# A third score tile in batch 0, proj on two other queues, and one-pass transposes in a hash-attention and max-out FFN kernel

## Chip, cores and metric

One core of one Trainium2 chip. The metric is device time in microseconds (us) of one launch; TensorE's granted clock is noted with each run, 1.000 being full speed. A ratio is always the mean time of one kernel's fast runs over the mean of the other's fast runs of the same rounds, so it is not quite the ratio of the medians quoted beside it. Brackets after a ratio are its 95% interval. Runs that the record marks as slow (over 1.5% above the fastest of the same kernel) are left out of ratios.

In the profiles PE is TensorE (PEld its weight loads), ACT is ScalarE, DVE is VectorE, POOL is GpSimd, and SP is SyncE, which here only issues DMAs. PSUM is the memory into which this kernel's matmuls write; its pools there are counted in banks, and a tile takes one or two of them.

## The reference

Attention in which a query sees only keys with the same 6-bit hash, then a feed-forward layer with the maximum of three products. 4 batches, 8 heads, 768 positions, 64 per head.

```python
q_bits = (np.einsum('bhsd,dk->bhsk', q, proj) > 0)      # 6 bits, k alike
mask = q_bucket[:, :, :, None] == k_bucket[:, :, None, :]
scores = np.where(mask, scale * np.matmul(q, k.transpose(0, 1, 3, 2)), -1e9)
attn = softmax(scores)                                   # + 1e-9 in the divisor
x = np.matmul(attn, v)                                   # to (3072, 512)
h = np.maximum(np.maximum(x @ w1, x @ w2), x @ w3)       # 512 -> 768
out = h @ w_out                                          # 768 -> 512
```

## The kernel before

The work goes pair of heads by pair of heads. I call the work on one pair of batch 0 a **stage**. A stage has twelve **score units** (two matmuls of 384 columns and one exp on ACT). Other work hangs on the numbered units of the stage: the row sums of the pair before ("den"), its output matmuls (`av`), the **hash** of the next pair, and the preparation of the pair after that. The FFN of a batch starts when its last pair is done, and its matmuls then fill TensorE between score units.

The hash bits get into the scores as extra rows of the score operands. Batch 0's first pair writes them with DVE; each later pair's hash goes into one tile, `bt`, from which eight small DMAs (9 KB each, all on SP's queue) carry it to the operand rows of the next stage.

```python
psp = tile_pool(name="psp", bufs=2, PSUM)   # score tiles, two banks each
psw = tile_pool(name="psw", bufs=4, PSUM)   # one-bank work tiles: all else

def hash_pair(b, j):
    bt = btp.tile([P, S], BF16, tag="bt", name="bt")
    ps = [bank(), bank()]                    # two work banks at once
    ...                                      # 8 matmuls over tf["q"], tf["k"]
    for half in (0, 1):
        nc.vector.tensor_scalar(out=bt[:, half_cols(half)], in0=ps[half][:, 0:HS], ...)
        for hd in (0, 1):
            for z, nm in enumerate(("q", "k")):
                o = 32 * (2 * (hd ^ half) + z)
                nc.sync.dma_start(oset(b, j)[nm, hd][HROW[hd] : HROW[hd] + 2 * NBITS, half_cols(half)],
                                  bt[o : o + 2 * NBITS, half_cols(half)])
```

The schedule of a stage `ph` (cut), where `add(u, f, ...)` hangs `f` behind score unit `u`:

```python
        if ph > 0:                                   # sparse: stages 1 to 4
            add(1, den_mm, ph - 1, 0, NT3 if sparse else NCH)
            if sparse:
                add(2, den_mm, ph - 1, NT3, NCH)     # ends in ACT's copy of the sums
            add(3 if sparse else 2, den_rc, ph - 1)  # DVE, then 8 small GpSimd copies "r"
            ...
        if ph == 1:
            for m in range(3):
                add(6, load_weight, m, 0)            # GpSimd's queue, 384 KB each
            add(6, load_v, 0, 2)
        else:
            add(6, load, "k", nb, nj)                # GpSimd's queue, 4 x 176 KB and more
            add(6, load, "q", nb, nj)
        ...
        if 0 < ph and ph + 1 < len(pairs):
            add(1, hash_pair, *pairs[ph + 1])
```

The softmax here doesn't subtract the row's maximum and nothing guards it: scores larger than these inputs give would overflow.

## Time and profile before

| | before |
|---|---|
| time | 301.68 us, median of 3 (300.83 to 303.58) |
| span of the profiled run, clock | 299.7 us, 0.998 |
| second exp of stages 1, 2, 3, 4 | 29.36, 42.96, 54.29, 65.77 us |
| first FFN matmul that needs the last pair | 73.26 us |
| from there to the end | 226.4 us, TensorE full |

All times in the trace count from the start of the span. I mark a stage by the start of its second exp, because the second score unit is the one that needs the seventh of the eight small DMAs.

### The profile page before, as it was taken

To read this page: it belongs to the slowest core of one execution; us is meant where nothing else is said; L and a number is where in the kernel's file an instruction comes from. 1 tells how busy PE (TensorE), PEld (TensorE's weight loads), DVE (VectorE), ACT (ScalarE), POOL (GpSimd) and SP (SyncE) were. 2 spreads that over 40 slices of the span, in tenths; PEclk is the share of its full clock that TensorE was granted. 3 is DMA by queue.
4 is the path that set the end of the run, shared out by engine and by line. 5 is a ranking of instruction groups with operands and counts; after the bars stand their busy time and mean duration, and the time that the engine had idled before them with its cause. 6 is when DMAs were issued, how large, how long until landed. Compare 5 with 4: busy or idle time off the path is not lost.

```text
span 299.7 us, 6326 instructions
## 1 busy us (share of the span) xinstructions
PE 281.5 (94%) x2328; PEld 147.7 (49%) x2328; DVE 196.4 (66%) x410; ACT 190.8 (64%) x286; POOL 101.5 (34%) x288
## 2 busy tenths in 40 slices
PE   6788888887999899999999999999999999999994
PEld 3344443333555345555555545554555455555551
DVE  2787576885888767887578858875787063725260
ACT  2456758877767696777767776768686966131322
POOL 8180506396344444435260717080202010100000
PEclk9999999999999999999999999999999999999999
DMA  7556193789979093909372757367202020020202
GB/s 238 159 153 131 15 181 88 149 186 199 230 136 200 19 232 121 194 11 218 114 195 35 171 164 173 58 148 188 38 0 37 20 88 1 2 105 0 108 0 106
DMA packets 21727, 34.56 MB, mean 115 GB/s; under 512 B 3744, under 2 KB 15936, under 8 KB 21696
## 3 DMA queue, kind: packets, MB, share of 16 engines
q0 software_dynamic: 14512, 23.60, 39.6%
q1 hardware_dynamic: 6496, 10.03, 9.6%
q10 hardware_dynamic: 688, 0.52, 0.5%
q8 instruction: 18, 0.29, 0.4%
q14 instruction: 13, 0.11, 0.1%
HBM read 33.03 MB, written 6.29 MB: 131 GB/s over the span
## 4 chain that ended last, share of the span: by engine, by line
PE 85%; ACT 6%; DVE 3%; issue 2%; DMA 2%; POOL 1%; ACTq 0%; DVEq 0%; POOLq 0%
PE wk L327 32%; PE sc L256 19%; PE wk L309 11%; PE wk L343 10%; PE wk L272 5%; PE wk L234 4%; PE wk L200 3%; DMA pr<-in_proj_dram 2%; PE wk L219 1%; DVE qtf L202 1%; ACT at_194 L258 1%; ACT at_201 L258 1%; ACT at_182 L258 1%; ACT at_181 L258 1%; ACT at_200 L258 1%
## 5 line engine op out<-in xcount | busy, mean ns | idle before, releaser
L327 PE MATMUL wk<-xT,w_sb 128*128 128x384 f16 x576 | 111.0, 326 | 0.7 <-DVE xT L315 0.7
L327 PEld LDWEIGHTS <-w_sb 128*128 128x128 f16 x576 | 54.1, 97 | 45.0 <-issue 9.8
L237 DVE TENSOR_SCALAR bt<-wk,thrqk,fac 128x384 bf16<-128x384 f32 x30 | 18.9, 673 | 22.3 <-PE wk L234 22.2
L256 PE MATMUL sc<-qop_0_165,kop_0_164 76*128 76x384 bf16 x72 | 23.6, 328 | 4.1 <-DVE qop_0_165 L223 0.6
L309 PEld LDWEIGHTS <-v 128*64 128x64 f16 x384 | 20.6, 110 | 13.7 <-issue 6.7
L91 POOL DMA_DIRECT2D qnat<-in_q_dram x48 | 26.5, 559 | 1.0 <-DMA v<-in_v_dram 1.0
L91 POOL DMA_DIRECT2D knat<-in_k_dram x48 | 26.4, 558 | 0.8 <-issue 0.8
L256 PE MATMUL sc<-qop_0_162,kop_0_160 128*128 128x384 bf16 x72 | 23.5, 326 | 0.4 <-DVE qop_0_162 L223 0.3
L256 PE MATMUL sc<-qop_1_171,kop_1_170 76*128 76x384 bf16 x60 | 19.7, 328 | 3.1 <-DMA kop_1_170<-bt 1.0
L357 ACT COPY o<-wk 128x512 f32<-128x512 f32 x23 | 13.5, 585 | 13.3 <-PE wk L343 13.2
L256 PE MATMUL sc<-qop_2_177,kop_2_176 76*128 76x384 bf16 x60 | 19.7, 328 | 2.2 <-ACT at_187 L258 0.6
L256 PE MATMUL sc<-qop_1_168,kop_1_166 128*128 128x384 bf16 x60 | 19.6, 326 | 0.1
L256 PE MATMUL sc<-qop_2_174,kop_2_172 128*128 128x384 bf16 x60 | 19.6, 327 | 0.0
L283 DVE STREAM_TRANSPOSE dT<-ds 128x384 f32<-128x384 f32 x16 | 9.2, 573 | 8.3 <-ACT ds L278 8.2
L258 ACT ACTIVATE at_185<-sc 128x768 f16<-128x768 f32 x8 | 6.5, 814 | 11.6 <-PE sc L256 11.6
L272 PEld LDWEIGHTS <-ones_154 128*32 128x32 f16 x384 | 8.6, 96 | 10.0 <-issue 6.9
L234 PE MATMUL wk<-qtf,pmq 64*32 64x384 f32 x120 | 13.4, 495 | 0.0
L234 PE MATMUL wk<-ktf,pmk 64*32 64x384 f32 x120 | 12.7, 495 | 0.0
L99 POOL DMA_DIRECT2D v<-in_v_dram x16 | 11.8, 739 | 1.7 <-PE sc L256 1.2
L312 DVE TENSOR_SCALAR sv<-wk 128x1 f32<-128x1 f32 x32 | 4.9, 152 | 11.4 <-PE wk L309 11.4
L256 PEld LDWEIGHTS <-kop_0_164 76*128 76x128 bf16 x72 | 7.0, 97 | 10.5 <-issue 5.3
L256 PEld LDWEIGHTS <-kop_0_160 128*128 128x128 bf16 x72 | 7.1, 98 | 9.9 <-issue 6.6
(479 smaller groups left out, 654.3 us busy)
## 6 DMA issues: line engine op xcount, KB each, us to landing
knat<-in_k_dram POOLq DMA_DIRECT2D x48, 176.0 KB, 4.0
qnat<-in_q_dram POOLq DMA_DIRECT2D x48, 176.0 KB, 5.2
out_dram<-o SPq DMA_DIRECT2D x7, 768.0 KB
v<-in_v_dram POOLq DMA_DIRECT2D x16, 192.0 KB, 5.4
w_sb<-in_moe_w_dram POOLq DMA_DIRECT2D x6, 384.0 KB, 6.8
wo_sb<-in_moe_w_out_dram POOLq DMA_DIRECT2D x1, 768.0 KB, 9.5
out_dram<-o SPq DMA_DIRECT2D x2, 256.0 KB
qnat_98<-in_q_dram ACTq DMA_DIRECT2D x2, 192.0 KB
```

Of the source, the lines that this page charges most:

```text
L91: nc.gpsimd.dma_start(t[32 * g : 32 * g + 32, :, 0 : NCH * D - 32], s[:, :, 32 * blk : 32 * blk + NCH * D - 32])
L99: nc.gpsimd.dma_start(t[:].rearrange("p h c d -> p h (c d)"), v[b, 2 * j : 2 * j + 2].rearrange("h (p c) d -> p h (c d)", p=P))
L234: nc.tensor.matmul(ps[half][o : o + 32, 0:HS], pm[nm][head_rows(hd), :], tf[nm, b, j][head_rows(hd), half_cols(half)], start=True, stop=True)
L237: nc.vector.tensor_scalar(out=bt[:, half_cols(half)], in0=ps[half][:, 0:HS], scalar1=thr["qk"][:, 0:1], scalar2=fac[:, 0:1], op0=AluOp.is_ ...
L256: nc.tensor.matmul(sc[:, hd, 0:HS], kT[rows, c * P : c * P + P], qT[rows, half * HS : half * HS + HS], start=True, stop=True)
L258: nc.scalar.activation(atile(ph, half, c)[:, :, 0:HS], sc[:, :, 0:HS], ActFn.Exp, scale=SCALE)
L272: nc.tensor.matmul(ps[32 * g : 32 * g + 32, 0:HS], ones32[:], atile(ph, half, c)[:, hd, 0:HS], start=(c == 0), stop=(c == NCH - 1))
L283: nc.vector.transpose(dT[:].rearrange("p a x -> p (a x)"), rcb.pop(ph)[:])
L309: nc.tensor.matmul(ps[D * hd : D * hd + D, 0 : HS + 1], vv[:, hd, c, :], atile(ph, half, c)[:, hd, :], start=(c == 0), stop=(c == NCH - 1))
L327: nc.tensor.matmul(ps[:, 0:HS], w_sb[m, fb // NT3][:, jc, (fb % NT3) * P : (fb % NT3) * P + P], xT[b][:, jc, half * HS : half * HS + HS], ...
L343: nc.tensor.matmul(ps[:, 0:DM], hts[b, half, fb][:, t * P : t * P + P], w_sb["o"][:, fb, :], start=(fb == 0), stop=(fb == NFB - 1))
L357: nc.scalar.copy(o[:, t, :], ps[:, 0:DM])
```

## The change

The intent: with two score tiles TensorE and ACT take turns; a third lets ACT keep work in hand in batch 0, where TensorE is not full. The two banks for it come from the work banks, and are given back (`split_scores`) in stage 4. Because only two work banks are left and the hash takes both, the hash moves from unit 1 to unit 3, behind the sums. proj no longer waits on GpSimd's queue. The transposes of pairs 1 to 3 become one pass over the full array, for which the two heads are loaded side by side, in pieces of 256 B.

```diff
-    psw = tile_pool(name="psw", bufs=4, PSUM)
+    psw = tile_pool(name="psw", bufs=2, PSUM)
+    extra = psx.enter_context(tc.tile_pool(name="psx3", bufs=1, PSUM))
+    sc_ring = deque((psp, psp, extra))       # three score tiles
+    def split_scores():                      # later: two score tiles, four banks
+        psx.close(); ...; bank_ring.extend((extra, extra))
 ...
     pr = konst.tile([P, NBITS], FP32, name="pr")
-    nc.gpsimd.dma_start(pr[0:D], proj[:, :])
-    nc.gpsimd.dma_start(pr[D : 2 * D], proj[:, :])
     for cs in (slice(0, NT3), slice(NT3, NCH)):
         load0("k", 0, nc.sync, cs)
         load0("q", 0, nc.scalar, cs)
+        if cs.start == 0:
+            nc.sync.dma_start(pr[0:D], proj[:, :])
+            nc.scalar.dma_start(pr[D : 2 * D], proj[:, :])
 ...                                          # pe_transpose, pairs 1 to 3
-            for hd in (0, 1):
-                nc.tensor.matmul(ps[head_rows(hd), c * P : c * P + P], nat[...][:, hd, o : o + D], iden[:], ...)
+                nc.tensor.transpose(ps[:, c * P : c * P + P], n[:, cc * P : cc * P + P], iden[:])
 ...                                          # schedule
+            if ph == NPAIR:
+                add(6, split_scores)
-            add(1, hash_pair, *pairs[ph + 1])
+            add(3 if ph <= NPAIR else 1, hash_pair, *pairs[ph + 1])
 ...                                          # stage 0; and prep of pairs 2, 3 on units 5, 7, 9, 10
-            add(3, hash_first, "q", 1)
-            add(3, convert, "q", 0, 0, h1)
-            add(4, hash_pair, 0, 1)
+            add(3, hash_pair, 0, 1)
+            add(4, hash_first, "q", 1)
+            add(4, convert, "q", 0, 0, h1)
```

More of the change, by code (lines that the diff above doesn't have):

```diff
@@ L60 @@
     psp = ctx.enter_context(tc.tile_pool(name="psp", bufs=2, space=bass.MemoryType.PSUM))
-    psw = ctx.enter_context(tc.tile_pool(name="psw", bufs=4, space=bass.MemoryType.PSUM))
+    psw = ctx.enter_context(tc.tile_pool(name="psw", bufs=2, space=bass.MemoryType.PSUM))
+    psx = ctx.enter_context(ExitStack())
     ctx.enter_context(tc.manual_schedule())
@@ L80, in load0 @@
         if (nm, 0, j) not in nat:
-            nat[nm, 0, j] = natp0.tile([P, 2, S // 2], FP32, tag=nm + "nat0", name=nm + "nat0")
+            nat[nm, 0, j] = natp0.tile([P, S], FP32, tag=nm + "nat0", name=nm + "nat0")
         src = HBM[nm][0, 2 * j : 2 * j + 2].rearrange("h (p c) d -> p h c d", p=P)[:, :, cs, :]
-        eng.dma_start(nat[nm, 0, j][:].rearrange("p h (c d) -> p h c d", d=D)[:, :, cs, :], src)
+        if j == 0:
+            eng.dma_start(nat[nm, 0, j][:].rearrange("p (h c d) -> p h c d", h=2, d=D)[:, :, cs, :], src)
+        else:
+            dst = nat[nm, 0, j][:].rearrange("p (c h d) -> p h c d", h=2, d=D)
+            for hd in (0, 1):
+                eng.dma_start(dst[:, hd, cs, :], src[:, hd, :, :])
     def load(nm, b, j):
@@ L180, in load_wo, with psum2 @@
         w_sb["o"] = t
-    def psum2(name):
-        return psp.tile([P, 2, 512], FP32, tag="ps", name=name)
+    extra = psx.enter_context(tc.tile_pool(name="psx3", bufs=1, space=bass.MemoryType.PSUM))
+    sc_ring = deque((psp, psp, extra))
+    bank_ring = deque((psw, psw))
+    def psum2():
+        sc_ring.rotate(-1)
+        return sc_ring[0].tile([P, 2, 512], FP32, tag="sc", name="sc")
     def bank():
-        t = psw.tile([P, 512], FP32, tag="wk", name="wk")
-        return t
+        bank_ring.rotate(-1)
+        t = bank_ring[0].tile([P, 512], FP32, tag="wk", name="wk")
+        return t
+    def split_scores():
+        psx.close()
+        extra = psx.enter_context(tc.tile_pool(name="psx1", bufs=2, space=bass.MemoryType.PSUM))
+        sc_ring.remove(sc_ring[[p is psp for p in sc_ring].index(False)])
+        bank_ring.extend((extra, extra))
     tf = {}
@@ L197, in pe_transpose @@
         for c in range(NT3):
-            o = (half * NT3 + c) * D
-            for hd in (0, 1):
-                nc.tensor.matmul(ps[head_rows(hd), c * P : c * P + P], nat[nm, b, j][:, hd, o : o + D], iden[:],
-                                 start=True, stop=True)
+            cc = half * NT3 + c
+            n = nat[nm, b, j]
+            if j == 0:
+                for hd in (0, 1):
+                    o = (hd * NCH + cc) * D
+                    nc.tensor.matmul(ps[head_rows(hd), c * P : c * P + P], n[:, o : o + D], iden[:],
+                                     start=True, stop=True)
+            else:
+                nc.tensor.transpose(ps[:, c * P : c * P + P], n[:, cc * P : cc * P + P], iden[:])
         evac(tf[nm, b, j][:, half_cols(half)], ps[:, 0:HS])
@@ L250, in qk_unit @@
     def qk_unit(ph, b, j, half, c):
-        sc = psum2("sc")
+        sc = psum2()
         for hd in (0, 1):
@@ L374 @@
     TAILW = 40.0
-    wps = psum2("wps")
+    wps = psum2()
     for _ in range(8):
@@ L398, in prep @@
             if nb == 0:
-                for i, (nm, half) in enumerate((("k", 0), ("k", 1), ("q", 0), ("q", 1))):
-                    add(u + i // 2, pe_transpose, nm, nb, nj, half, nc.vector.tensor_copy)
+                for u, nm, half in ((5, "k", 0), (7, "k", 1), (9, "q", 0), (10, "q", 1)):
+                    add(u, pe_transpose, nm, nb, nj, half, nc.vector.tensor_copy)
                     if half == 1:
-                        add(u + i // 2, convert, nm, nb, nj)
+                        add(u, convert, nm, nb, nj)
             else:
@@ L419 @@
         if ph == 0:
-            add(2, hold, nat["q", 0, 1][:, 0, 0:1])
+            add(2, hold, nat["q", 0, 1][:, 0:1])
             add(2, load_v, 0, 0)
```

## The prediction

> **What bounds the kernel now.** I read the page first, then the table by stretches, the timeline of TensorE and SP, the waits of PE, and the chain that ended last in order of time. The page says who is full:
>
> ```profile
> PE 281.5 (94%) x2328; PEld 147.7 (49%) x2328; DVE 196.4 (66%) x410; ACT 190.8 (64%) x286; POOL 101.5 (34%) x288
> PE   6788888887999899999999999999999999999994
> ```
>
> One digit is 7.5 us. From the tenth digit on TensorE is full; before that it is at seven or eight tenths. I cut the table by stretches at the first score matmul of each pair (a "stage" is one pair of heads of batch 0) and at the first FFN matmul. Columns: stretch, its length, then busy time and count of PE, PEld, DVE, ACT, POOL, the clock, DMA share, GB/s.
>
> ```profile
> 11.27:27.89 16.62, 14.55 (x157) 7.96 (x157) 13.73 (x27) 9.06 (x12) 6.85 (x11) 1.00 0.65 155
> 27.89:41.66 13.77, 12.28 (x136) 6.45 (x137) 8.74 (x19) 8.98 (x14) 4.38 (x12) 1.00 0.46 69
> 41.66:52.96 11.30, 9.41 (x89) 3.86 (x89) 6.78 (x15) 9.26 (x14) 5.59 (x16) 1.00 0.59 118
> 52.96:64.44 11.48, 9.55 (x89) 3.86 (x89) 8.91 (x18) 9.29 (x14) 6.56 (x18) 1.00 0.71 150
> 64.44:73.26 8.82, 7.02 (x70) 2.65 (x69) 7.02 (x14) 6.20 (x9) 6.25 (x16) 1.00 1.21 205
> 73.26:290.00 216.74, 215.69 (x1712) 116.94 (x1712) 144.48 (x284) 142.19 (x217) 64.27 (x178) 1.00 0.45 106
> ```
>
> From 73.26 on, when batch 0 is finished and its FFN fills every gap, PE is busy 215.69 of 216.74 us, and the change leaves that work alone. So the question is only how much earlier than 73.26 the first FFN matmul starts. Before it no engine is full: in stages 2 and 3 PE, DVE and ACT are all below 84%. The cause is two score tiles: PE waits for an exp, then goes off to other work, and ACT runs dry. The timeline of PE and of ACT in stage 2:
>
> ```profile
> 46.70 0.32 PE L256 MATMUL sc<-qop_2_177,kop_2_176 76*128 76x384 bf16 x1 [0.61 <-ACT at_181 L258]
> 47.99 0.81 ACT L258 ACTIVATE at_184<-sc 128x768 f16<-128x768 f32 x1
> 49.52 0.81 ACT L258 ACTIVATE at_185<-sc 128x768 f16<-128x768 f32 x1 [0.72 <-PE sc L256]
> ```
>
> Exps back to back start 0.71 us apart; the gap after the one at 47.99 is the 1.11 us of output matmuls that PE had put between two score units. At the front the chain is different: everything waits for proj.
>
> ```profile
> 1.94 5.37 DMA pr<-in_proj_dram
> 7.43 0.47 DVE pmq L139
> 7.94 0.35 DVE ktf L202
> 8.34 0.86 PE wk L219 x4
> 13.55 1.46 PE wk L200 x24
> ```
>
> The k half that DVE evacuates at 7.94 was in PSUM at about 5.6 (its transposes start at 4.72 and take 0.88); DVE stood behind pm, which stood behind proj.
>
> **What the Trainium skill says.** (1) "DMA: Bandwidth & Descriptors", Specifications: first byte about 1 us for a GpSimd-issued DMA and about 0.6 us for one from SP or ACT, and at least 512 B for line rate. The first agrees in direction only: proj took 5.37 us because it shared engines with the loads that ran at over 300 GB/s from 3 to 9 us. The second bears on the new loads, whose pieces fall from 1536 to 256 B; no row of this trace shows what that costs. (2) "TensorEngine Tiling (Array Packing)", Restrictions: column tiling disables the transpose mode of fp32 input. The transposes now write halves of 64 partitions and the trace shows two passes per matmul (24 instructions for 12 matmuls), as that would have it. (3) "Perfetto Trace Analysis", Transposes: use the transpose, not a standard matmul. This trace has none to compare. (4) The same page, Identifying Dependency Chains: consistent bubbles can mean too few buffers; the ACT gaps above, repeated in each stage at the same place, agree.
>
> **The change, part by part.**
>
> *Front.* proj now goes out as the second DMA on SP and on ACT, behind the first k and q halves, whose transposes start at 4.72. I take it to land at 5.0. pm is then done by 5.6, ktf leaves at 5.65 instead of 7.94, and hashing starts near 6.25 instead of 8.34: 2.1 us earlier, all on the path.
>
> *Transposes.* 12 matmuls of two passes per k or q of a pair become 6 transposes. At the 61 ns per pass seen now (1.46 us over 24) that is 0.37 us with one pass each and 0.73 us with two. PE drops 0.7 to 1.1 us for each of six such groups, 4.4 to 6.5 us in all, but most of it lies where PE waits for DVE or ACT, so I do not add it; it only keeps PE from becoming the bound.
>
> *Third score tile.* With three, ACT has up to two units in hand while PE does 1.11 us of output matmuls or 1.4 us of den and hash. The floor of a stage is then ACT: 12 exps at 0.71 plus one 0.36 us copy, about 9.0, so PE/ACT alternation would give 9.0 to 9.8 us instead of 11.3 to 13.8.
>
> *What pays for it.* Two work banks instead of four until the split. So the hash, which needs two, moves from unit 1 to unit 3 and waits for ACT's copy of the sums. That lengthens another chain, which SP shows:
>
> ```profile
> 45.04 0.72 SPq L243 DMA_DIRECT2D qop_0_165<-bt  x1
> ...
> 49.84 0.72 SPq L243 DMA_DIRECT2D qop_0_162<-bt  x1
> 50.61 0.72 SPq L243 DMA_DIRECT2D kop_0_160<-bt  x1
> ```
>
> Each hash sends eight small DMAs, 0.78 us apart, and the second score unit of the next stage needs the seventh. From the first issue that is 6 x 0.78 + 0.72 = 5.4, and 1.4 to landing (stage 1 began 1.4 us after the end of such an issue): 6.8. Directly measured at stage 0: first issue 21.73, second unit of stage 1 at 28.46, that is 6.73. Now the loop from a stage's second unit: score 0.33, den 0.6, score 0.33, den 0.6, the copy of the sums ends 2.5; rest of the hash 0.7; DVE does dT and rc before bt (to 3.6) and the first bt half to 4.25; first issue 4.35; plus 6.8. That is 11.1 us per stage, more than the ACT floor. Before, the hash at unit 1 closed this loop in about 9.6 and the alternation in 11.4 hid it.
>
> *Sum, by the second score unit of each stage.* Stage 1 before: 28.46. After: 2.1 from the front, and about 1.9 since pair 1's hash now stands ahead of the second q half's hash and converts on DVE (2 x 0.6 + 0.7): 24.5, gain 4.0. Stage 2 before: 42.37, 13.9 later; after 11.3 (the 11.1 plus a little, as pair 3's four groups share two banks with the output matmuls): gain 2.6. Stages 3 and 4: 11.34 and 11.48 become 11.1: gain 0.6. From stage 4's second unit to the first FFN matmul: 8.1 before; 2.5 to the copy plus the 4.8 of dT, rc, GpSimd copies, rb and xT seen from 68.41 to 73.22: 7.3, gain 0.8. Total 8.0, so 301.7 - 8.0 = 293.7.
>
> **The rivals.** *The small-DMA chain does not bind* (landing quicker, hash earlier): stages run at the ACT floor plus stalls, about 9.8. Three stages then give 3 x 1.3 more: about 289.8. For it: exps and PE have the room. Against it: SP's spacing of 0.78 is in every stage, and the order of the after kernel has the hash wait for ACT. *Two banks choke it:* each evacuation waits in DVE's line behind converts (0.55 each) and rb, and DVE is already busy 13.73 of 16.62 in stage 0. If every stage loses 1 us more, the gain is about 4: 297.7. *Loads in 256 B pieces starve stage 0:* pairs 1 and 2 are 1.57 MB; at the 350 GB/s of now they land by 9, at half of it by 15. k of pair 1 is needed near 11.3 and pair 2 not before 17, so a halving hides; at a third of the rate stage 0 slips by 2 us or so: 296. *Nothing is kept:* GpSimd and DMA (share 1.21 just before the FFN) set when weights and batch 1 arrive, and an earlier FFN could wait for them. Against it: GpSimd's work of a stage is 6.6 us of 11.1, and PE shows three waits, 1.1 us in all, on other engines after 73 us.
>
> **Range and chances.** I take 293.6. The low end, 289.5, is the first rival; the high end, 297.5, is choked banks or slow loads. A gain of over 2% means under 295.6; the sum leaves 2 us of room to that and its parts have an error of about 2.5 us together, so 0.75 faster, 0.24 within 2%, and 0.01 slower, as no part touches the full stretch after 73 us.
>
> **What would show it.** Right: proj landed near 5 us and first hash matmul near 6.2; first FFN matmul near 65.3; stages 2 and 3 near 11 us with PE's first waits there on the bt DMAs; PE busy down by 4 to 6 us; the stretch from the first FFN matmul to the end still 226.4 us. Wrong in its main step: stages 2 and 3 under 10.3 us (the DMA loop does not bind), or over 11.5 with PE waiting for DVE at den, hash or output matmuls (two banks bind), or the first transposes of pair 1 waiting for a load (pieces bind), or a longer stretch after the FFN begins.

## The result

312.95 us (median of 4, 311.23 to 315.05) against 302.00 (median of 4) before: ratio 1.0362 [1.0279, 1.0445]. The kernel became 3.6% slower. All runs after are at a clock of 0.953 to 0.965. The profiled one has a span of 311.8 us.

The page of the kernel after, the same two lines as before and the clock (before, that row shows 9 in all forty places):

```profile
PE 286.9 (92%) x2220; PEld 145.8 (47%) x2220; DVE 196.2 (63%) x410; ACT 192.1 (62%) x286; POOL 100.3 (32%) x286
...
PE   8786969494999989999999999999999999999994
...
PEclk9997887687799999999999999999999999999998
```

PE has 108 instructions fewer, yet is busy 5.4 us longer: for a part of batch 0 it ran at a lower clock. In the second row TensorE now drops to 4 in two places, and the clock falls around the same places.

The table by stretches, cut as before at the first score matmul of each stage (same columns: stretch, length, busy and count of PE, PEld, DVE, ACT, POOL, clock, DMA share, GB/s):

```profile
9.97:27.48 17.51, 12.14 (x87) 5.88 (x85) 13.77 (x27) 9.21 (x12) 7.18 (x12) 0.97 0.96 188
27.48:41.09 13.61, 12.97 (x101) 5.40 (x101) 7.50 (x17) 8.88 (x12) 4.59 (x12) 0.78 0.33 45
41.09:55.82 14.73, 11.85 (x89) 3.96 (x88) 6.82 (x15) 9.15 (x13) 5.84 (x17) 0.77 0.60 111
55.82:71.28 15.46, 11.34 (x89) 4.16 (x88) 8.98 (x18) 9.68 (x14) 5.59 (x16) 0.78 0.49 102
71.28:84.60 13.32, 8.51 (x67) 2.50 (x66) 7.27 (x15) 7.31 (x10) 6.60 (x16) 0.74 1.00 174
84.60:311.00 226.40, 222.05 (x1742) 119.89 (x1741) 146.57 (x288) 144.10 (x221) 64.30 (x179) 1.00 0.43 103
```

The last cut, 84.60, is the very first FFN matmul. The cut at 73.26 before was the fourth, the first that needs the last pair; after, that one starts at 85.08. Like for like, the FFN starts 11.8 us later, and from there to the end of the span it is 311.8 - 85.08 = 226.7 us, 226.4 before. So all but 0.3 us of the loss lies in batch 0. Stages 2 and 3 take 14.73 and 15.46 us instead of 11.30 and 11.48, the stretch from stage 4 to that fourth matmul 13.80 instead of 8.82. (Stage 1 looks unchanged only because the cut falls at its first score unit, ahead of the wait; by second exps it went from 13.6 to 15.6.) The mean clock in these stretches is 0.74 to 0.78.

What holds them? The chain of work that ended last, cut to batch 0 (start, length, what), names the same thing once in each stage:

```profile
21.15 7.03 DMA kop_1_172<-bt
...
39.52 5.03 DMA qop_2_180<-bt
44.59 0.48 PE sc L282
45.07 1.08 PE wk L298 x12
...
55.78 5.14 DMA qop_0_168<-bt
...
71.57 5.03 DMA qop_1_174<-bt
```

These are the small hash DMAs. In the chain before they do not occur at all in stages 2 to 4. The line at 45.07 is half of the row sums of a pair: 1.08 us. The same group took 0.60 before:

```profile
29.12 0.60 PE wk L272 x12
```

So TensorE is near half speed just after it stood waiting. The waits of PE after, the longest first (us in total, times, longest); before, no wait for the small DMAs was over 1.0 us:

```profile
PE sc L282 <- DMA kop_1_176<-bt: 2.7, 1, 2.7
PE sc L282 <- DMA kop_1_172<-bt: 2.3, 2, 1.9
```

**Why 5 us for 9 KB?** Lay SP's timeline beside GpSimd's. SP after, the first small DMA of stages 1 and 2 (start, length of the issue):

```profile
34.89 0.72 SPq L269 DMA_DIRECT2D qop_2_183<-bt  x1
...
50.98 0.72 SPq L269 DMA_DIRECT2D qop_0_171<-bt  x1
```

GpSimd's timeline after, the big loads of the same stages, and below it GpSimd's before:

```profile
35.84 2.25 POOL L181 DMA_DIRECT2D w_sb<-in_moe_w_dram  x3
...
51.41 2.22 POOL L97 DMA_DIRECT2D knat<-in_k_dram  x4
```

```profile
48.81 2.22 POOL L91 DMA_DIRECT2D knat<-in_k_dram  x4
```

Before, stage 2's first small DMA went out at 45.04 (shown in the prediction), 3.8 us ahead of the loads. After, it goes out at 50.98, only 0.4 us ahead, and the other seven run into them. Both now follow the copy of the sums. From 42 to 45 us the DMA share is 1.3 and 200 GB/s move. Stage 1's seventh, issued at 39.52, needs 5.1 us from there to the matmul that waits for it.

The kept traces also hold each DMA packet with its queue, start and length (`prof` only sums them). They show where the 5 us go. The seventh small DMA of stage 2 is issued at 55.78. Its packets, counted in order of start, begin only between 59.16 and 60.05, behind those of the six before it, while packets of GpSimd's queue run without a pause from 52.7 to 60.8. Once begun, no data packet of these eight DMAs takes over 0.11 us. So the time is a wait before the packets start, not a slow write.

At the front, proj moved as intended (timeline of the first 13 us; the bracket is what ended the idle time):

```profile
4.72 1.54 PE L224 MATMUL wk<-iden,knat_94 128*64 128x128 f32 x12
5.44 0.71 DVE L146 COPY pmq<-pr 128x6 f32<-128x6 f32 x1 [2.00 <-DMA pr<-in_proj_dram]
...
6.92 0.84 PE L245 MATMUL wk<-ktf,pmk 64*32 64x384 f32 x4
```

proj landed before 5.44 instead of 7.3, the first hash matmul started at 6.92 instead of 8.34, and stage 0's scores at 9.97 instead of 11.27. Pair 1's first small DMA left at 18.62 instead of 21.73. But its loads (from 16.39) met these DMAs too: the chain's first line above, 7.03 us. Stage 1 begins no earlier than before (second exp 29.53 against 29.36).

### The profile page after: what moved, and what is told of

It is laid out like the page before. It is cut to its first block, busy times and chain, and to the rows that moved or that the text cites.

```text
span 311.8 us, 6096 instructions
## 1 busy us (share of the span) xinstructions
PE 286.9 (92%) x2220; PEld 145.8 (47%) x2220; DVE 196.2 (63%) x410; ACT 192.1 (62%) x286; POOL 100.3 (32%) x286
## 3 DMA queue, kind: packets, MB, share of 16 engines
q1 hardware_dynamic: 14352, 10.03, 11.2%
## 4 chain that ended last, share of the span: by engine, by line
PE 83%; DMA 9%; DVE 4%; ACT 2%; SPq 1%; issue 1%; ACTq 0%
PE wk L353 30%; PE sc L282 19%; PE wk L369 10%; PE wk L335 10%; PE wk L298 7%; PE wk L260 5%; DMA qop_2_180<-bt 3%; DMA kop_1_172<-bt 2%; DMA qop_0_168<-bt 2%; DMA qop_1_174<-bt 2%; PE sc L404 1%; PE wk L224 1%; SPq L269 1%; DVE bt L263 1%; DVE ktf L228 1%; PE wk L245 1%
## 5 line engine op out<-in xcount | busy, mean ns | idle before, releaser
L335 PEld LDWEIGHTS <-v 128*64 128x64 f16 x384 | 20.7, 110 | 13.6 <-issue 6.4
L282 PE MATMUL sc<-qop_0_168,kop_0_166 128*128 128x384 bf16 x72 | 24.0, 334 | 3.2 <-DMA kop_0_166<-bt 1.6
L282 PE MATMUL sc<-qop_0_171,kop_0_170 76*128 76x384 bf16 x72 | 24.0, 333 | 3.0 <-DVE qop_0_171 L238 0.8
L282 PE MATMUL sc<-qop_1_174,kop_1_172 128*128 128x384 bf16 x60 | 20.9, 348 | 4.0 <-DMA kop_1_172<-bt 2.3
L282 PE MATMUL sc<-qop_1_177,kop_1_176 76*128 76x384 bf16 x60 | 20.9, 348 | 3.6 <-DMA kop_1_176<-bt 2.7
L282 PE MATMUL sc<-qop_2_180,kop_2_178 128*128 128x384 bf16 x60 | 20.2, 336 | 2.7 <-DMA kop_2_178<-bt 2.0
L383 ACT COPY o<-wk 128x512 f32<-128x512 f32 x23 | 13.5, 585 | 13.3 <-PE wk L369 13.2
L282 PE MATMUL sc<-qop_2_183,kop_2_182 76*128 76x384 bf16 x60 | 20.3, 338 | 0.0
L260 PE MATMUL wk<-qtf,pmq 64*32 64x384 f32 x120 | 15.0, 530 | 0.0
L260 PE MATMUL wk<-ktf,pmk 64*32 64x384 f32 x120 | 13.7, 529 | 0.0
L105 POOL DMA_DIRECT2D v<-in_v_dram x16 | 12.1, 754 | 3.3 <-DMA knat<-in_k_dram 3.3
L282 PEld LDWEIGHTS <-kop_0_170 76*128 76x128 bf16 x72 | 7.0, 98 | 12.1 <-issue 5.9
L338 DVE TENSOR_SCALAR sv<-wk 128x1 f32<-128x1 f32 x32 | 4.9, 154 | 11.3 <-PE wk L335 11.1
L234 DVE STREAM_TRANSPOSE qtf<-qnat 128x768 f32<-128x768 f32 x12 | 11.7, 975 | 0.2
```

Source lines behind the costliest of these rows:

```text
L105: nc.gpsimd.dma_start(t[:].rearrange("p h c d -> p h (c d)"), v[b, 2 * j : 2 * j + 2].rearrange("h (p c) d -> p h (c d)", p=P))
L234: nc.vector.transpose(dst.rearrange("p (c pg i) -> p c pg i", pg=4, i=32), src)
L260: nc.tensor.matmul(ps[half][o : o + 32, 0:HS], pm[nm][head_rows(hd), :], tf[nm, b, j][head_rows(hd), half_cols(half)], start=True, stop=True)
L282: nc.tensor.matmul(sc[:, hd, 0:HS], kT[rows, c * P : c * P + P], qT[rows, half * HS : half * HS + HS], start=True, stop=True)
L335: nc.tensor.matmul(ps[D * hd : D * hd + D, 0 : HS + 1], vv[:, hd, c, :], atile(ph, half, c)[:, hd, :], start=(c == 0), stop=(c == NCH - 1))
L383: nc.scalar.copy(o[:, t, :], ps[:, 0:DM])
```

## The experiments

**The theory** after reading the traces: the hash at unit 3 makes the small DMAs run beside GpSimd's loads; that makes their landing 3 us longer, and TensorE, idle there, falls to half clock. **Rivals:** two work banks hold up TensorE, whatever the order; half clock is the main cost, not a follow-up; the 256 B pieces or the third tile itself do harm; landing is slow for another reason, such as SP's own queue.

"Second exps" are those of stage 1, then the distances from stage 1 to 2, 2 to 3, 3 to 4. "FFN" is the first FFN matmul that needs the last pair. From there to the end of the span it is 226.1 to 226.9 us in all profiles but one (e2: 228.5), so the FFN's start tells nearly everything.

| run | ratio to before | clock, fast runs | second exps | FFN |
|---|---|---|---|---|
| before | 1 | .987 to 1.0 | 29.36; 13.6, 11.3, 11.5 | 73.26 |
| after | 1.0362 | .953 to .965 | 29.53; 15.6, 16.4, 15.7 | 85.08 |
| e1 hash ahead of sums | 1.0189 | .959 to .972 | 27.76; 14.8, 10.7, 13.8 | 77.74 |
| e2 loads held back | 1.0035 | .983 to .994 | 27.09; 13.0, 10.9, 12.2 | 74.06 |
| e3 before, hash at 3 | 1.0334 | .973 to .983 | 30.38; 13.8, 14.8, 16.0 | 83.65 |
| e4 no third tile | 0.9885 | .994, .999 | (profile slow) | |
| e5 warm-up matmuls | 1.0289 | .993 to 1.0 | 29.89; 14.6, 15.7, 15.4 | 83.16 |
| e6 e1 without third tile | 1.0073 | .974 to .989 | 26.88; 11.6, 11.3, 12.1 | 73.09 |
| e7 proj alone | 0.9952 | .992 to 1.0 | 28.84; 13.6, 11.3, 11.5 | 72.71 |
| e8 transposes alone | 0.9967 | .981 to .994 | 28.52; 13.5, 11.3, 12.3 | 74.23 |
| e9 e6 with warm-up | 0.9965 | .993 to 1.0 | 27.95; 13.4, 12.3, 12.4 | 73.47 |
| e10 e1 with loads held | 1.0031 | .975 to .989 | 26.57; 13.3, 10.7, 13.6 | 74.34 |
| e11 e10 with warm-up | 1.0104 | .999, 1.0 | 28.38; 15.0, 12.5, 12.6 | 76.71 |
| e12 proj and order | 0.9906 | .998 to 1.0 | 27.24; 13.8, 11.3, 11.7 | 71.50 |

A warning on the quoted expectations: where one gives times of stages of an earlier run, I had at that time counted some exps twice at the edges of neighbouring stretches of the timeline, which makes some stages seem shorter (e2's stage 2 at 9.6 us, for one). The table is a recount.

**e3: the kernel before, with nothing but the hash moved.**

```diff
-            add(1, hash_pair, *pairs[ph + 1])
+            add(3 if ph <= NPAIR else 1, hash_pair, *pairs[ph + 1])
```

> The kernel before with one part of the change alone: its hash moved from unit 1 to unit 3 in stages 1 to 4. Four work banks, two score tiles, old transposes, old proj. Theory (the later hash is what costs): stages 1 to 3 go to 14 to 16 us, with PE waiting for the small DMAs, and the time rises by 6 to 12 us, to 308 to 314. Rival A (two banks choke, the move itself is harmless): the time stays within 2 us of 302.

312.44 us (310.19 to 313.66), 1.0334 [1.026, 1.0408]. Two score tiles, four banks, old transposes, old proj, and nearly the whole loss: the FFN starts 10.4 us later than before. Its chain:

```profile
38.64 5.07 DMA qop<-bt
...
53.09 5.28 DMA qop<-bt
...
69.06 5.32 DMA qop<-bt
```

This alone shows that neither the third tile, nor the bank count, nor the 256 B pieces is needed for the loss. The move of the hash alone is enough.

**e2: the changed kernel, loads of stages 0 to 3 held until the hash rows are there.** A one-column copy on GpSimd stands ahead of the loads; it reads the operand rows that the seventh of the eight small DMAs writes.

```diff
+                add(9, hold, oset(*pairs[ph + 1])['q', 1][:, HS : HS + 1])
-                add(6, load, "k", nb, nj)      # and the weights, v
+                add(9, load, "k", nb, nj)
```

> The changed kernel with the big GpSimd loads of stages 0 to 3 held back until the hash rows of the next pair have landed (a copy of one column on GpSimd waits for the seventh of the eight small DMAs). The hash stays at unit 3. Theory (small DMAs land 5 us after issue because of the loads, 2.1 us without them): the stage falls by some 3 us to about 12 and most of the half-clock windows go, since the gap before the score units shrinks under 2 us; time 298 to 304. Rival A (two banks choke): no change, over 309. Rival C (landing is slow for another reason, such as the issue ring of SP): the landing stays near 5 us, stages over 15, time over 309.

303.49 us (302.2 to 304.5, 20 runs), 1.0035 [1.0011, 1.0059]. About ten of the eleven us come back. Its chain, the seventh small DMA of stages 2 and 3:

```profile
48.72 1.84 DMA qop<-bt
...
60.88 1.84 DMA qop<-bt
```

1.84 us against 5.1, with the same hash, the same tile count and the same banks: the loads are what makes the landing slow. The packets agree: those of stage 2's seventh begin 1.4 us after its issue, and GpSimd's queue is idle from 47.7 to 52.5. (The first four of the same eight, issued from 43.93 on, still stood behind the held loads of the stage before and began only from 47.3 on.) Stage 4 now starts 2.6 us earlier than before (63.18 against 65.77), but the FFN 0.8 us later. PE's waits show where it goes:

```profile
PE wk L353 <- DVE xT L341: 4.3, 1, 4.3
```

GpSimd's `r` copies of stage 4, which xT needs, stand behind the held loads in GpSimd's order (loads from 63.3, the first `r` at 70.9). The hold moves a wait from one stage to another.

**e1: the changed kernel, the hash put back to unit 1, ahead of the sums**, so that two banks suffice.

```diff
+            if sparse:
+                add(1, hash_pair, *pairs[ph + 1])     # ahead of den_mm
             add(1, den_mm, ph - 1, 0, ...)
-            add(3 if ph <= NPAIR else 1, hash_pair, *pairs[ph + 1])
```

> The changed kernel with one move undone in spirit: in stages 1 to 4 the hash of the next pair runs at unit 1 ahead of the two den groups, not at unit 3 behind them, so it no longer waits for ACT's copy of the sums. Everything else, the two work banks and the third score tile too, stays. Theory (the loop from hash through eight small DMAs to the next stage's second score unit is what sets the stage, and its DMAs land late because they run into GpSimd's big loads): the first of the eight goes out about 2.5 us sooner, ahead of those loads, so stages fall from 15.6 to about 11 to 12 us, PE has no gap of 2 us or more before the score units, the half-clock windows go, and the time is 294 to 300 us. Rival A (two work banks choke the stages): the stages stay at 14 us or more, now with PE waiting for DVE at den or at the output matmuls, and the time stays over 307. Rival B (the throttled clock is the cause by itself, from the transposes): the half-clock windows stay and the time stays over 307.

307.72 us, 1.0189 [1.0119, 1.0259]. About half of the loss is gone, and PE waits for the small DMAs of batch 0 only 1.1 us in all. Its longest waits are others:

```profile
PE sc L282 <- ACT at L284: 4.1, 10, 1.5
PE wk L298 <- DVE bt L263: 3.6, 4, 1.1
...
PE wk L260 <- DVE qtf L234: 2.8, 2, 1.4
```

The first is ten waits of score units for an exp. The second is the row sums waiting for a bank that the hash still holds: the two-bank rival, real now. The third is a wait for data: the hash, so early, is ahead of DVE's transposes of the next batch.

**e6: e1 with two score tiles and four banks.** Against e1 it is a clean test of the third tile with its price in banks.

```diff
-    psw = bufs=2 ... sc_ring = deque((psp, psp, extra)) ... add(6, split_scores)
+    psw = bufs=4 ... sc_ring = deque((psp, psp))
```

> The kernel of two score tiles and four work banks (as the fourth run) with the hash at unit 1 ahead of the den groups in stages 1 to 4 (as the first run). Against the first run it differs only in the third score tile and the two banks it takes. If the two banks are what holds the first run at 307.7: 294 to 299 here, no PE wait for DVE at den. If the third tile gains as its intent says: slower here than the first run by some us. Against the fourth run: the small DMAs go out about 0.7 us sooner, 0 to 2 us better per run, with the same clock.

304.13 us (301.09 to 305.95, 9 runs), 1.0073 [1.003, 1.0116]; three of the nine runs are slow. Without the third tile the FFN starts 4.7 us earlier than in e1. Only the distance from stage 2 to 3 was shorter with it (10.7 against 11.3). So the tile bought with two banks costs more than it brings; a part of that is half clock, which e1 has more of (17 us against 13.6 in the profiles). Stage 4 starts 3.8 us earlier than before here, yet the FFN only 0.2. The clock row and the stretch in question:

```profile
PEclk9998999966999999999999999999999999999998
```

```profile
62.00:72.00 10.00, 9.23 (x62) 2.78 (x62) 4.99 (x10) 5.06 (x7) 5.04 (x14) 0.50 1.18 196
```

Ten us at half clock with PE busy for 9.23 of them: here, unlike in the kernel after, TensorE bounds, and half clock takes what the stages had won. (The profiled run, 301.09 us, is the fastest of the nine, so the others lose more than it shows.)

**e5: the changed kernel with eight warm-up matmuls ahead of the first two score units of stages 1 to 4**, to keep the clock up and see what it costs.

```diff
+        if 1 <= ph <= NPAIR and c == 0:
+            for _ in range(8):
+                nc.tensor.matmul(sc[:, 0, :], warm[:, 0:P], warm[:], start=True, stop=True)
```

> The changed kernel with eight warm-up matmuls (zeros, 0.22 us each) into the score tile ahead of each of the first two score units of stages 1 to 4, where TensorE otherwise stands still and waits for the small DMAs. It takes away the idle time, not the wait. If the half-clock windows (four of 6.8 us in the changed kernel) are a further cost on the loop, caused by that idleness: fewer or none of them, den, scores and hash run at full speed after the wait (1.5 us less per stage), stages near 14 us, time 306 to 310. If the clock only looks bad and costs nothing on the path: time stays 311 to 315 with a clock near 1. If the windows come from the transposes and not from idleness: they stay.

310.49 us, 1.0289 [1.0237, 1.034], clock 0.993 to 1.0. With the clock nearly whole, about 2 us come back, and the intervals of this ratio and of the one without filler overlap. The warm-up costs 1.73 us for eight on the path itself, so the 2 us alone are only a lower bound on the price of the clock. From stage 2 to 4, however, its chain holds no filler (it fits into the waits), and even so the two distances fell only by 0.7 and 0.3 us. The chain tells why:

```profile
53.64 6.12 DMA qop<-bt
...
69.17 5.98 DMA qop<-bt
```

In these two stages the small DMAs go out 1.1 to 1.7 us sooner after the second exp (4.1 to 4.2 us instead of 5.3 to 5.8) and then take about 1 us longer to land. What the clock gave, the loads took again. Here half clock is a follow-up, not the cause.

**e4: the changed kernel without the third tile, four banks, hash at its old unit.**

```diff
-    psw = bufs=2 ... sc_ring = deque((psp, psp, extra)) ... add(6, split_scores)
+    psw = bufs=4 ... sc_ring = deque((psp, psp))
-            add(3 if ph <= NPAIR else 1, hash_pair, *pairs[ph + 1])
+            add(1, hash_pair, *pairs[ph + 1])
```

> The changed kernel without its third score tile: two score tiles and four work banks all the way, hash at unit 1 behind the first den group as in the kernel before. It keeps proj on SP and ACT, the one-pass transposes, their 256 B loads and the new places of the preparation. Theory: the front's gain and the shorter transposes stay and the small-DMA loop closes in under 11.4 us, so 296 to 300 us. Rival D (the 256 B loads or the transposes are what costs): over 305 us.

301.86 us median of 4: 296.59 and 300.62 fast, 303.1 and 304.4 slow; 0.9885 [0.9771, 0.9999] over the two fast ones, unclear. It bears out that the loss goes with the third tile and its hash move, and holds the fastest single run of all; four runs so far apart say no more.

**e7: the kernel before with proj on SP and ACT alone.**

```diff
-    nc.gpsimd.dma_start(pr[0:D], proj[:, :])        # and the other half
+            nc.sync.dma_start(pr[0:D], proj[:, :])
+            nc.scalar.dma_start(pr[D : 2 * D], proj[:, :])
```

> The kernel before with one part alone: proj on SP and ACT, behind the first k and q halves. Working of the prediction: hashing starts 2.1 us sooner and the whole of batch 0 moves with it, 299.5 to 300.5. Rival: the start of stage 1 is set by the small DMAs of pair 1 that run into GpSimd's loads, which do not move with it, and the gain is under 1 us.

300.57 us (20 runs), 0.9952 [0.9933, 0.9972]: a gain of 1.4 us. In the profiled run every stage and the FFN start 0.5 us earlier, and the distances are those of before.

**e8: the kernel before with the new loads and transposes alone** (the hunks of `load0` and `pe_transpose`).

> The kernel before with one part alone: pairs 1 to 3 loaded head by head in 256 B pieces and transposed by six full-array transposes per k or q. PE saves 0.9 to 1.1 us in each of six groups (the changed kernel shows 0.49 us per three). If PE was on the path there: 297 to 300. If the waits for DVE and the small DMAs set stages 0 and 1: within 1 us of 302. If the 256 B loads are too slow: slower than 302.5, with PE waiting for a load at the first transposes.

300.73 us (20 runs), 0.9967 [0.994, 0.9993]: a gain of about 1.0 us. So the 256 B pieces do no harm that outweighs it. But all 20 runs had a clock of 0.981 to 0.994. Its three runs at 0.981 to 0.983 took 302.9 to 303.8 us, the six at 0.993 or 0.994 took 300.0 to 300.7. The kernel before lost clock less often: of its 42 fast runs in the same rounds 25 had 0.997 or more. That TensorE, with less work where it is not the bound, became idle enough to lose clock is a guess; no run tells it from an effect of the new transposes themselves.

**e9: e6 with two or three warm-up matmuls at the borders of stages, in a work bank.**

```diff
+        fill = 2 if (ph == 0 and u > 6) or (0 < ph < NPAIR and u > 8) else 3 if 1 <= ph <= NPAIR and u < 2 else 0
+        if fill:
+            wps = bank()
+            ... # fill warm-up matmuls
```

> The sixth run (two score tiles, four banks, hash ahead of the sums) with two or three warm-up matmuls into a free work bank ahead of the score units at the stage borders, where TensorE stands. In the sixth run the profile showed 13.6 us at half clock, 10.2 of them just as the FFN began at 62 us. If idleness brings the half clock there and the half clock costs: clock 0.995 or more, stage 4 to the FFN back to 8 us, 294 to 298 us. If the half clock is not from idleness: it stays and the time stays near 304. If fill costs what it saves: 300 to 302.

301.75 us (12 runs), 0.9965 [0.9935, 0.9996], clock 0.993 to 1.0. The 294 to 298 us hoped for did not come, but the filler saved more than it cost: e6 has 1.0073 [1.003, 1.0116], so e9 is about 1% faster, and the intervals lie apart. At full clock the stretch from stage 4 to the FFN takes 7.4 us, in e6 11.2. Against that, stage 4 starts 4.2 us later than in e6's profiled run (66.08 against 61.92).

**e10: e1 with the loads of stages 0 to 2 held as in e2; e11: e10 with warm-up matmuls in the score tile.** I meant them to join e1's and e2's gains.

```diff
+            if ph < NPAIR - 1:
+                add(9, hold, oset(*pairs[ph + 1])['q', 1][:, HS : HS + 1])   # e10, with the hash of e1
+        for _ in range(fill):
+            nc.tensor.matmul(sc[:, 0, :], warm[:, 0:P], warm[:], ...)        # e11, fill as in e9
```

> The changed kernel, third tile and two banks kept, with both cures: hash at unit 1 ahead of the sums, and the big loads of stages 0 to 2 held until the hash rows have landed. Stage 3 is not held, since holding it put GpSimd's copies for the reciprocals behind the loads and cost 4 us at the FFN's start in the second run. Theory: with the small-DMA loop out of the way the third tile does what it is for, stages 1 to 3 take 9.5 to 10.5 us (the second run's stage 2 took 9.6), the FFN starts near 67 us, 295 to 299 us, with some half-clock windows in it. If two banks choke stages even so: stages of 11.5 us or more and 302 or more.

> The tenth run with two or three warm-up matmuls in the score tiles of the border units. If its half-clock windows cost: 2 to 4 us below the tenth run, 292 to 296. If fill delays the score units more than it gives: equal or slower than the tenth run.

e10: 303.43 us, 1.0031 [1.0012, 1.005]; e11: 305.57 us, 1.0104 [1.0067, 1.0142]. Both miss. In e10 the row sums wait 3.9 us for the bank of the hash and the hash 2.9 us for DVE's transposes, as in e1, so the third tile with two banks does not pay even with the DMAs in order. e11 has the full clock and is slower than e10; its row sums wait 3.2 us for the same bank. That the filler ahead of its score units is what delays it is likely, but not shown.

**e12: the kernel before with proj on SP and ACT and the change's new order of preparation in stages 0 and 1**; old transposes, two score tiles, four banks, hash at unit 1.

```diff
+            nc.sync.dma_start(pr[0:D], proj[:, :])                # and ACT
-                    add(u + i // 2, pe_transpose, nm, nb, nj, half, nc.vector.tensor_copy)
+                for u, nm, half in ((5, "k", 0), (7, "k", 1), (9, "q", 0), (10, "q", 1)):
+            add(3, hash_pair, 0, 1)
+            add(4, hash_first, "q", 1)
```

> The kernel before with proj on SP and ACT and the changed kernel's order of the preparation in stages 0 and 1 (pair 1's hash ahead of the second q half's, the transposes of pairs 2 and 3 at units 5, 7, 9 and 10). Old two-pass transposes and whole-row loads, two score tiles, four banks, hash at unit 1. The seventh run, proj alone, gave 300.6 and its stage 1 began only 0.5 us sooner than before, held by the small DMAs of pair 1. If pair 1's hash is what held it: stage 1 begins 2 us sooner or more, 297 to 299.5 us, with the clock near 1 since TensorE has as much work as before. If the loads hold the small DMAs whenever they start: 300 to 301, as the seventh.

299.88 us (299.34 to 300.34, 6 runs) against 303.17 on the same chip: 0.9906 [0.987, 0.9942], clock 0.998 to 1.0. It beats both kernels, the one before by 0.9%. Stage 1 starts 2.1 us earlier and the FFN 1.8; the distances between stages are within 0.2 us of before. It holds the parts of the change that lengthen nothing and leave TensorE its work.

## Why the prediction was wrong

It said 293.6 us, 0.01 for slower. By its own steps:

**The bound of the changed stages: right.** It named the loop "hash, eight small DMAs, second score unit of the next stage" as what would bind after the change, and the chain after shows it in each stage. The sum of 11.1 us was right too, for the conditions it took. e2 gives them in stage 2: from its second exp at 40.08 to the first issue at 43.93 is 3.85 us, to the seventh at 48.72 another 4.79, then 1.84 to landing, and 0.46 to the next second exp at 51.02: 10.9 us. (Its other two distances, 13.0 and 12.2 us, are lengthened by the hold itself, which delays GpSimd's `r` copies.)

**The step that failed: "1.4 to landing".** The prediction took it from the border of stages 0 and 1 of the kernel before, where the last of these DMAs were issued as GpSimd's loads ran out. It held for DMAs that run beside no load. In the changed kernel the seventh needs 5.03 to 5.14 us from issue to landing in stages 1 to 3, where the prediction has 0.72 + 1.4 = 2.1. The trace before held a warning: in its stage 1 the seventh, issued at 35.95, also ran into loads, and its packets began only between 39.78 and 40.75. There it was not needed until 42.37, so no wait showed it. The working had the cause in hand: it moved the hash behind ACT's copy of the sums, but did not ask what else waits for that copy. GpSimd's `r` copies do, and behind them, in program order, the loads. The fourth rival spoke of loads against an earlier FFN, not against the hash.

**What it left out: the clock.** The prediction held the clock at 1.00 throughout. The half clock lengthens den (1.08 us instead of 0.60) and hash in the loop. By second exps, the distance from stage 1 to 2 after: 5.36 to first issue, 4.63 to the seventh, 5.07 to the matmul, 0.58 to the exp, 15.6 in all. The prediction's own loop in these terms is 3.9, 4.7, 2.1 and 0.45, 11.15 in all. So of 4.5 us too little, 3.0 are the landing and 1.5 the slow start; the three distances, 15.6, 16.4 and 15.7, foreseen as 11.3, 11.1 and 11.1, together miss 14.2. e5 shows that the second term would not have come back by itself.

The Trainium skill, "TensorE: Matmul & The Clock Gate", Part 1, says that the clock goes to half after an idle window of about 3.4 us and back after a busy one, with windows that run free of the kernel; "Why this matters for your kernels" there asks for no idle gaps over about 3 us. This case agrees on the halving and the size of the windows: the half-clock stretches at 43.7 to 50.5 and 57.4 to 64.1 are 6.8 us, twice 3.4. On the gaps it differs. Two windows of 3.4 us that ended as the clock fell (columns as above):

```profile
40.40:43.80 3.40, 1.44 (x8) 0.75 (x9) 1.98 (x4) 1.50 (x2) 0.00 (x0) 0.98 1.33 206
...
71.10:74.50 3.40, 0.70 (x3) 0.14 (x3) 3.27 (x6) 2.07 (x4) 3.40 (x5) 0.98 1.04 226
```

PE was busy for 42% and 21% of them, and no single wait in them was over 2.0 us. In e6 the window before the fall at 62.0 is fuller still:

```profile
58.60:62.00 3.40, 2.12 (x10) 0.77 (x8) 3.29 (x6) 3.05 (x6) 3.40 (x7) 0.99 1.03 237
```

There PE was busy for 62%, and no wait was over 0.7 us. The measurement decides: short gaps, close together, were enough here. A threshold does not come out of these traces.

**The front: right in mechanism, short in size.** proj landed near 5.4, not 5.0, and hashing began at 6.92, not 6.25, as the first transposes took 1.54 us instead of the 0.88 assumed (in this profile the clock rose to full only at 6.1 us, in that before at 4.7). But "gain 4.0" at stage 1 failed by the same step: its 6.8 us from first issue to second unit became 10.0 (18.62 to 28.58). e12, which keeps the front, has 2.1 us of it.

**The transposes: right.** One instruction each, 108 fewer in all, no wait of PE for the new loads; and rightly not added to the gain. They start 0.11 us apart, so six take about 0.66 us, near the 0.73 that the prediction had for two passes.

**The rivals.** "Small-DMA chain does not bind" is wrong. "Two banks choke it" is not what happened in the changed kernel, but it is what kept e1 and e10 from recovering. "256 B pieces starve stage 0" is not seen. The sum closes within half a microsecond: the FFN was foreseen at 65.3 and its matmul started at 85.08, 19.8 us later, and the time misses by 312.95 - 293.6 = 19.35. Of the 19.8, roughly 5 are stage 1's start, 14 the three distances and 1 the way from stage 4 to the FFN. Two misreadings did no harm: TensorE's row before is full from the eleventh digit, not the tenth, and 73.26 is the fourth FFN matmul, not the first (71.89).

**Left open.** The packets show that a 9 KB transfer beside loads waits before it starts, but not by what rule it gets its turn. The Trainium skill, "DMA: Bandwidth & Descriptors", Queues, rings and completion order, says that each DMA engine takes turns between its queues, a whole packet at a time. SP's small DMAs are on another queue than GpSimd's loads, and the traces agree with such a sharing (1.84 us in e2 against 5.1, short packets that start late); the packet records that were kept do not name the engine, so the order of turns is not shown. Nor is it shown what the third tile would bring if it cost no banks.

## What to carry to other kernels

Before moving an instruction, list what else is released by the event that it now waits for: two streams that were apart by accident of order can fall together, and a small transfer that sits on the critical path should not share the engines with bulk loads. A latency read from one place in the trace holds for the traffic at that place; check the DMA share there and where you mean to use it. And in a stage that TensorE doesn't bound, cutting its work brings little (e8: 0.3%); look at the granted clock before and after.

## What the Trainium skill lacked or had wrong

- "DMA: Bandwidth & Descriptors", Queues, rings and completion order: it tells the rule by which engines share queues, but gives no figure for a small transfer beside bulk loads on another queue. Here 9 KB took 1.84 us alone (e2) and 5.0 to 5.3 us beside loads (after, e3), 7.0 at worst.
- "TensorE: Matmul & The Clock Gate", Why this matters for your kernels: "No PE-idle gaps >~3µs" is too loose as a rule. The clock fell to half after windows of 3.4 us in which PE was busy for 0.70 and 1.44 us with no wait over 2.0 us, and in e6 after one with 2.12 us and no wait over 0.7. Another section of that page does say that frequent short idles can bring the clock down, but gives no figure for them.
- The same page, Part 1: it does not say what warm-up work costs in a kernel with waits. Eight warm-up matmuls took 1.73 us on the path (e5). Filler gained about 1% in e9 over e6, and lost 0.7% in e11 against e10.
- "Perfetto Trace Analysis", Transposes: its advice to use the transpose is borne out in count (2328 to 2220 PE instructions), but it does not say that the gain needs TensorE to be the bound: e8, where waits bind the stages, gained 0.3%.
